# Attention with sinks and an ELU feed-forward on one core: another shape for the sinks' product, another place for one subtraction, and two operations that ScalarE may take

## The chip, the cores and the metric

One core of one Trainium2 chip. The metric is the device time of one execution in microseconds (us); below it is the median of several runs. TensorE (PE) multiplies, VectorE (DVE), ScalarE (ACT) and GpSimd (POOL) do the element work, SyncE (SP) issues the transfers.

## The reference

```python
# q, k, v: 4 batches x 8 heads x 768 positions x 64; n_sink 4, window 128
scores = scale * np.matmul(q, k.transpose(0, 1, 3, 2))
keep = is_sink | in_window            # 4 sinks, and the last 128 positions
a = np.exp(scores - max); a = a / (sum + 1e-09)
x = matmul(a, v)                      # tokens (4 x 768 = 3072) x 512
h = x @ w_in                          # 512 x 2048
g = np.where(h > 0.0, h, np.exp(np.minimum(h, 0.0)) - 1.0)
return g @ w_out                      # 2048 x 512
```

## The kernel before

The 3072 tokens are 24 tiles of 128, taken in nine chunks of 2, 2, 2 and then 3 tiles. A tile sees its own keys, those of the tile before it and, from the third tile of a batch on ("far"), the four sinks. For each chunk the four pairs of heads go through attention, which leaves x, and then 16 blocks f of the hidden layer go through the feed-forward. The order of the parts is: blocks 0 to 7 of chunk 0, blocks 0 to 7 of chunk 1, blocks 8 to 15 of chunk 0, blocks 8 to 15 of chunk 1, then all 16 blocks of each further chunk. The attention of a chunk runs between the blocks of the chunks ahead of it.

Numbers are kept in two 16-bit parts, a high and a low one, so a product takes three matmuls. In `feed_forward` the first product of a block (L783, "S1") is 12 matmuls into one half-used PSUM bank `h`; there are two such banks. ScalarE takes the exponential (L791) into `g` in SBUF, VectorE subtracts one and scales (L793), VectorE takes the larger of that and h (L794) into `g`, ScalarE rounds it to the high part `gh` (L796), GpSimd subtracts to get the low part `gl` (L797), and the second product (L804, "S2", 6 matmuls for two tiles) adds into the banks `acc`. The bank `h` is free for the second block after when L794 is done; S2 of a block stands some two blocks behind its S1.

The weights come as 32 pieces of 64-bit words `raw` that are turned into 32-bit numbers on the chip: ScalarE scales the upper word into the bank `acc` that is not yet in use (L274), the sign (L277 on VectorE or L275 on GpSimd) and the low bits (L278 on VectorE or L276 on GpSimd) go into `wu`, VectorE puts them together (L279), ScalarE rounds the high part (L428) and GpSimd subtracts for the low part (L429).

Chunks 0 and 1 have an attention of their own in 32-bit numbers, `attention_f32`: scores (L505, 64 rows for each head), the masked maximum (L512, VectorE), the exponential (L515, ScalarE), four turns on TensorE (L522, "turn"), the copy of the turned probabilities to `pt` (L526, ScalarE or VectorE), then in `values` the product with the values (L562) and a product that spreads the reciprocal of the sum (L568); these two write 64 rows of the bank `po` for each head. Chunk 1 alone of these is far: two small turns (L547) bring the sinks' eight columns into `po`, L550 copies them to eight rows of a `pq` tile, and L565 multiplies these 8 rows with 128 columns, both heads at once, between L562 and L568. Behind `values`, L581, L582, L584 and L585 make x, its high part on ScalarE and its low part on VectorE; the next S1 needs all four pairs. Chunk 2 and later have another attention (scores L679 in chunk 2, L673 and L674 later; values L743 and L748).

No order is written by hand: `Plan` holds every task with an engine (some with a second one), a duration, what it depends on, and, for TensorE, a position. `forward` places tasks engine by engine, the most urgent first, each at the engine that takes it earliest; what comes out is the order in which each engine's queue is recorded.

Of the kernel before, what the change touches and what calls it, by code (L numbers as in the profile page):

```python
# [45 lines left out]
LAG = 2  # L46
WHOLE = 3
# [3 lines left out]
RINGS = dict(kqs=2, kq=3, vs=2, vm=1, vhl=2, e=3, st=6, pq=3, pt=6, g=2, gh=3, x=7, wv=4, s=2, po=1, h=2, wu=2, sv=2, wps=1, raw=6, s4=4, tp=2, rx=2)  # L51
# [44 lines left out]
class Plan:  # L96
# [6 lines left out]
    PATIENCE, LEEWAY, ISSUED = 0.1, 5.0, 0.15  # L103

# [3 lines left out]
    def add(self, eng, dur, fn, *args, deps=(), lat=0.0, pos=None, or_=None, gap=1.75, port=None):  # L108

        t = Task(eng, dur, fn, args, deps, lat, pos, gap, port)  # L110
        if or_:
            t.ways[or_[0]] = or_[1:]
        self.tasks.append(t)
        return t
# [59 lines left out]
    def forward(self):  # L174
# [6 lines left out]
        lock = 0.0  # L181
# [11 lines left out]
        while done < len(self.tasks):  # L193
# [61 lines left out]
def dve_us(n):  # L255
    return 0.1 + 0.00104 * n
# [10 lines left out]
def weight_f32(nc, v, d, u, raw):  # L267
# [8 lines left out]
        "bits POOL": lambda: nc.gpsimd.tensor_scalar(ui[:, :, 0], halves[:, :, 1], 2.0**-13, -4095.5 / 8192, ALU.mult, ALU.add),  # L276
        "sign DVE": lambda: nc.vector.tensor_scalar(ui[:, :, 1], halves[:, :, 3], 0x8000, None, ALU.bitwise_and),  # L277
# [52 lines left out]
def fast_path(tc, ctx, first, kq, vx, wt, out, nw, flag, limits):  # L330
# [71 lines left out]
    def weights(k):  # L402
# [8 lines left out]
        def step(i):  # L411
            return lambda: weight_f32(nc, v, acc[2], wu[k % RINGS["wu"]], raw)[i]()

        ld = add("SP", 0.45, load, deps=[w_done.get(k - AHEAD, [None])[0]], lat=dma_us(P * 512 * 8))
        if wide:
            a = add("ACT", act_us(512) + 0.05, step("d"), deps=[ld])
            u1 = add("DVE", 0.34, step("sign DVE"), deps=[ld], or_=("POOL", 0.75, step("sign POOL")), port=True)
            u2 = add("DVE", 0.34, step("bits DVE"), deps=[u1], or_=("POOL", 0.85, step("bits POOL")), port=True)
# [45 lines left out]
    def attention_f32(c):  # L464
# [12 lines left out]
        for p in range(NP):  # L477
# [10 lines left out]
            for j, g in enumerate(ts):  # L488
# [18 lines left out]
                sc = add("PE", 0.75 if c else 0.65 if nb == 1 else 1.2, scores, deps=[ldk, *freed] if c and k < 1 else [ldk], pos=at[k])  # L507
# [33 lines left out]
            sk_ = sp = None  # L541
            if far:
                sp = pqs[slot("pq")].rearrange("p b k -> p (b k)").bitcast(F32)[0 : 2 * NS, :qc]
# [5 lines left out]
                sk_ = add("PE", 0.3, sinks, deps=[u for v in prods for u in (v[0], v[9])], pos=at[k - 1] + 2.5)  # L549
                cs = add("ACT", act_us(qc) - 0.03, lambda sp=sp, po=po: nc.scalar.activation(sp, po[0 : 2 * NS, :qc], AF.Copy), deps=[sk_], or_=("DVE", dve_us(qc) - 0.03, lambda sp=sp, po=po: nc.vector.tensor_copy(sp, po[0 : 2 * NS, :qc])))  # L550
# [3 lines left out]
            def values(po=po, vr=vr, sp=sp, prods=prods):  # L554
                for _, _, _, pt, rs, g, j, nb, _, _ in prods:
# [8 lines left out]
                    if far:  # L564
                        nc.tensor.matmul(po[:, oc], vr[0 : 2 * NS, nk * P : (nk + 1) * P], sp[:, oc], start=False, stop=False)  # L565
# [4 lines left out]
            val = add("PE", 0.2 + sum(0.22 * v[7] + 0.22 for v in prods), values, deps=[ldv, sk_, *[u for v in prods for u in v[:2]]], pos=at[k - 1] + 4.0)  # L570
# [3 lines left out]
            if far:  # L574
                ring("pq", [sk_], [val])
# [16 lines left out]
    def attention(c):  # L592
# [39 lines left out]
        for p in range(NP):  # L632
# [21 lines left out]
            for g in ts:  # L654
# [29 lines left out]
                else:  # L684
                    scs = [add("PE", 0.75, scores([0, 1]), deps=kqp[0][2:4], pos=at[k])] * 2
# [27 lines left out]
                if t >= 2:  # L713
# [8 lines left out]
                    b = add("POOL", 0.85, sinks, deps=[rr], port=False)  # L722
# [27 lines left out]
            val = add("PE", 0.16 + sum(0.16 * v[4] + (0.06 if v[5] >= 2 else 0.0) for v in prods), values, deps=[va, vb, *[v[0] for v in prods]], pos=at[k - 1] + V_AT)  # L750
# [4 lines left out]
            fa = add("ACT", act_us(qc), lambda xh=xh, po=po: nc.scalar.activation(xh, po[:, :qc], AF.Copy, scale=PO_SCALE), deps=[val])  # L755
            fb = add("DVE", dve_us(qc), lambda xh=xh, xl=xl, po=po: nc.vector.scalar_tensor_tensor(xl, po[:, :qc], PO_SCALE, xh, ALU.mult, ALU.subtract), deps=[fa])
# [375 lines left out]
```

## Time and profile before

| | us |
|---|---|
| median of 3 runs | 639.59 |
| lowest and highest | 638.42, 641.27 |
| profiled execution, its own time | 636.94 |
| its span, first to last instruction | 634.9 |
| TensorE busy in the span | 613.5 (97%) |
| VectorE, ScalarE, GpSimd busy | 429.7, 416.0, 366.1 |

The span is read in stretches: the attention of chunk 0 up to the first S1 at 30.8 us; the first part of chunk 0 with the attention of chunk 1 up to 76.7 us, where the first S1 of chunk 1 starts; the two parts behind it; the steady rest up to 628.2 us, and a tail. In the timeline's rows a matmul of 32-bit numbers counts as two instructions.

### The profile page before, as it was taken

To read this page: it belongs to the slowest core of one execution; us is meant where nothing else is said; L and a number is where in the kernel's file an instruction comes from. 1 tells how busy PE (TensorE), PEld (TensorE's weight loads), DVE (VectorE), ACT (ScalarE), POOL (GpSimd) and SP (SyncE) were. 2 spreads that over 40 slices of the span, in tenths; PEclk is the share of its full clock that TensorE was granted. 3 is DMA by queue.
4 is the path that set the end of the run, shared out by engine and by line. 5 is a ranking of instruction groups with operands and counts; after the bars stand their busy time and mean duration, and the time that the engine had idled before them with its cause. 6 is when DMAs were issued, how large, how long until landed. Compare 5 with 4: busy or idle time off the path is not lost.

```text
span 634.9 us, 13430 instructions
## 1 busy us (share of the span) xinstructions
PE 613.5 (97%) x4521; PEld 373.6 (59%) x4521; DVE 429.7 (68%) x1202; ACT 416.0 (66%) x1181; POOL 366.1 (58%) x617
## 2 busy tenths in 40 slices
PE   5799899999999999999999999999999999999995
PEld 3566566677776565555656565565555555555552
DVE  6989897777869666576666777676676967442222
ACT  5977878668888766666676766666667666432221
POOL 3778777865778665555656666655546674222221
PEclk9999999999999999999999999999999999999998
DMA  8764993555665754364535565464345624300001
GB/s 311 262 251 171 265 250 137 164 151 147 142 160 121 180 118 118 98 178 120 149 102 143 153 117 155 108 202 120 118 113 150 191 69 106 88 35 17 0 2 55
DMA packets 113517, 87.94 MB, mean 139 GB/s; under 512 B 88352, under 2 KB 93472, under 8 KB 113440
## 3 DMA queue, kind: packets, MB, share of 16 engines
q1 hardware_dynamic: 113296, 87.00, 49.4%
q8 instruction: 37, 0.61, 0.4%
q14 instruction: 40, 0.33, 0.2%
q10 hardware_dynamic: 144, 0.00, 0.0%
HBM read 58.41 MB, written 7.34 MB: 104 GB/s over the span
## 4 chain that ended last, share of the span: by engine, by line
PE 91%; DVE 4%; ACT 2%; issue 1%; DMA 1%; POOL 0%; DVEq 0%; ACTq 0%
PE h L783 39%; PE acc L804 39%; PE po L743 4%; PE s L674 3%; PE s L673 3%; ACT e L515 1%; DMA words<-in_words_dram 1%; PE po L562 1%; DVE wv L279 1%; DVE e L512 1%; DVE wu L278 1%; PE s L679 1%; PE po L565 1%; PE po L748 0%; PE po L568 0%
## 5 line engine op out<-in xcount | busy, mean ns | idle before, releaser
L783 PE MATMUL h<-x,w 128*128 128x384 f16 (+1 forms) x1728 | 273.2, 309 | 1.3 <-DVE g L794 1.3
L783 PEld LDWEIGHTS <-w 128*128 128x128 f16 x1728 | 164.4, 98 | 91.1 <-issue 2.7
L797 POOL TENSOR_TENSOR gl<-g,gh 128x384 f16<-128x384 f32 (+1 forms) x144 | 126.3, 878 | 155.0 <-ACT gh L796 120.4
L804 PE MATMUL acc<-w,gh 128*128 128x512 f16 x768 | 192.7, 380 | 0.0
L793 DVE TENSOR_SCALAR g<-g 128x384 f32<-128x384 f32 (+1 forms) x144 | 64.1, 445 | 122.5 <-ACT g L791 121.9
L796 ACT ACTIVATE gh<-g 128x384 f16<-128x384 f32 (+1 forms) x144 | 69.4, 482 | 76.5 <-DVE g L794 76.2
L804 PEld LDWEIGHTS <-gh 128*128 128x128 f16 x768 | 70.2, 98 | 70.6 <-issue 1.6
L710 DVE SCALAR_TENSOR_TENSOR pq<-e,st,pq 128x256 f16<-128x256 f32 x160 | 88.3, 583 | 33.9 <-ACT pq L709 33.5
L791 ACT ACTIVATE g<-h 128x384 f32<-128x384 f32 (+1 forms) x144 | 64.5, 448 | 69.9 <-PE h L783 60.1
L804 PE MATMUL acc<-w,gl 128*128 128x512 f16 x384 | 109.2, 379 | 0.1
L697 ACT ACTIVATE e<-e,st 128x264 f32<-128x264 f32 x160 | 78.0, 488 | 11.4 <-DVE st L695 9.8
L709 ACT ACTIVATE pq<-e,st 128x256 f16<-128x256 f32 x160 | 69.6, 479 | 6.9 <-DVE st L702 3.9
L794 DVE SCALAR_TENSOR_TENSOR g<-g,h 128x384 f32<-128x384 f32 (+1 forms) x144 | 72.3, 503 | 2.0
L695 DVE CUSTOM_DVE_ANT_0 e<-s,m 128x264 f32<-128x264 f32 x160 | 60.4, 405 | 13.7 <-PE s L674 12.4
L624 POOL TENSOR_TENSOR kq<-kqs,kq 128x396 fp32r<-128x396 f32 (+1 forms) x48 | 58.2, 1213 | 13.0 <-ACT kq L621 8.0
L804 PEld LDWEIGHTS <-gl 128*128 128x128 f16 x384 | 37.6, 98 | 45.8 <-POOL gl L797 0.6
L621 ACT ACTIVATE kq<-kqs 128x780 fp32r<-128x780 f32 (+1 forms) x48 | 42.7, 901 | 16.3 <-PE s L674 12.3
L625 POOL TENSOR_TENSOR kq<-kqs,kq 64x384 fp32r<-64x384 f32 x48 | 48.2, 1004 | 3.8
L673 PE MATMUL s<-kq 128*128 128x264 f32 (+1 forms) x144 | 50.0, 366 | 0.0
L701 POOL TENSOR_SCALAR st<-st 128x2 f32<-128x2 f32 x80 | 17.4, 218 | 43.4 <-ACT e L697 36.3
L429 POOL TENSOR_TENSOR w<-wv,w 128x512 f16<-128x512 f32 x32 | 38.3, 1197 | 5.6 <-ACT w L428 3.5
L674 PE MATMUL s<-kq 128*128 128x264 f32 (+1 forms) x144 | 37.8, 282 | 0.0
(120 smaller groups left out, 696.1 us busy)
## 6 DMA issues: line engine op xcount, KB each, us to landing
raw<-in_wt_dram SPq DMA_DIRECT2D x32, 512.0 KB, 5.4
kqs<-in_kq_dram SPq DMA_DIRECT2D x24, 456.0 KB, 3.5
kqs<-in_kq_dram SPq DMA_DIRECT2D x24, 390.0 KB, 3.2
out_dram<-wv SPq DMA_DIRECT2D x24, 256.0 KB, 2.9
vs<-in_vx_dram SPq DMA_DIRECT2D x20, 256.0 KB, 2.9
vm<-in_vx_dram SPq DMA_DIRECT2D x6, 768.0 KB, 4.7
vs<-in_vx_dram SPq DMA_DIRECT2D x12, 320.0 KB, 3.1
kqs<-in_kq_dram SPq DMA_DIRECT2D x8, 326.0 KB, 4.2
```

Source lines behind the costliest of these rows:

```text
L673: nc.tensor.matmul(sp[:, :wd], q, hi[:, c0 : c0 + wd], start=True, stop=False)
L695: red = add("DVE", 0.08 + 0.00104 * wd, lambda ee=ee, me=me, sp=sps[e], m=m, wd=wd: nc.vector.tensor_tensor_reduce(ee, sp[:, :wd], m[:, :w ...
L697: ex = add("ACT", act_us(wd, sums=True), lambda ee=ee, me=me, rs=rs[:, e : e + 1]: nc.scalar.activation(ee, ee, AF.Exp, bias=me, scale=-1. ...
L709: a = add("ACT", act_us(nb * P, True), lambda src=src, hi=hi, re=re: nc.scalar.activation(hi, src, AF.Copy, scale=re), deps=[rr])
L710: b = add("DVE", dve_us(nb * P) + 0.03, lambda src=src, hi=hi, lo=lo, re=re: nc.vector.scalar_tensor_tensor(lo, src, re, hi, ALU.mult, ALU ...
L783: nc.tensor.matmul(hp[:, :n], win[:, part, d, :], xx[:, :n], start=k == 0, stop=k == 3 * ND - 1)
L791: a = add("ACT", act_us(n) + 0.06, lambda gf=gf, hp=hp, sums=sums: nc.scalar.activation(gf, hp[:, :n], AF.Exp, scale=1.0 / G_SCALE, accum_ ...
L793: b = add("DVE", 0.07 + 0.00053 * n, lambda gf=gf: nc.vector.tensor_scalar(gf, gf, -1.0, G_SCALE, ALU.add, ALU.mult), deps=[a], port=True)
L794: b = add("DVE", dve_us(n), lambda gf=gf, hp=hp: nc.vector.scalar_tensor_tensor(gf, gf, 0.0, hp[:, :n], ALU.min, ALU.max), deps=[b])
L796: th = add("ACT", act_us(n), lambda gf=gf, gh=gh: nc.scalar.activation(gh[:, :n], gf, AF.Copy), deps=[b])
L797: tl = add("POOL", pool_us(n), lambda gl=gl, gf=gf, gh=gh: nc.gpsimd.tensor_tensor(gl[:, :n], gf, gh[:, :n], ALU.subtract), deps=[th])
L804: nc.tensor.matmul(acc[i], gg[:, i * P : (i + 1) * P], wout[:, part, :], start=f == f0 and k == 0, stop=f == f1 - 1 and k == 2)
```

## The change

1. In chunk 1 the sinks' eight rows are copied into the first 8 rows of a 128-row tile `sq` of zeros (two of them, cleared at the start by GpSimd), and the sinks' product is two matmuls of 128 rows by 64 columns, one for each head, of the same form as those beside it.
2. For chunk 0 (`NEAR`), L794 writes its result into the unused half of the bank `h` in place of `g`; ScalarE rounds from there, and VectorE in place of GpSimd subtracts from there for `gl`. The bank `h` is free only behind that subtraction, the tile `g` already behind the maximum.
3. ScalarE may take g's scaling (in all chunks) and the weights' low bits.
4. The planner's durations are renewed, and a matmul whose shape (`mode`) differs from that of the task ahead costs it 0.096 us more.

```diff
+NEAR = 1
+            if e == "PE":
+                s, mode = s + (self.SWITCH if t.mode != mode else 0.0), t.mode
...
+        "bits ACT": lambda: nc.scalar.activation(ui[:, :, 0], halves[:, :, 1], AF.Copy, scale=2.0**-13, bias=-4095.5 / 8192),
...
+    sqs = rows("sq", [P, SIZES[1] * P], F32)
+    for t in sqs:
+        nc.gpsimd.memset(t, 0.0)
...
-            u2 = add("DVE", 0.34, step("bits DVE"), deps=[u1], or_=("POOL", 0.85, step("bits POOL")), port=True)
+            u2 = add("DVE", 0.34, step("bits DVE"), deps=[u1], or_=[("POOL", 0.85, step("bits POOL")), ("ACT", 0.56, step("bits ACT"))], port=True)
...
-                        nc.tensor.matmul(po[:, oc], vr[0 : 2 * NS, nk * P : (nk + 1) * P], sp[:, oc], start=False, stop=False)
+                        for e in range(2):
+                            vo = nk * P + e * D
+                            nc.tensor.matmul(po[e * D : (e + 1) * D, oc], vr[:, vo : vo + D], sq[:, oc], start=False, stop=False)
...
+            near = 2 * n <= 512 and c < NEAR
+            gd = hp[:, n : 2 * n] if near else gf
+            if near:
+                tl = add("DVE", dve_us(n) - 0.035, lambda gl=gl, gd=gd, gh=gh: nc.vector.tensor_tensor(gl[:, :n], gd, gh[:, :n], ALU.subtract), deps=[th])
+                ring("h", [s1], [tl])
+            else:
+                tl = add("POOL", pool_us(n), lambda gl=gl, gd=gd, gh=gh: nc.gpsimd.tensor_tensor(gl[:, :n], gd, gh[:, :n], ALU.subtract), deps=[th])
+                ring("h", [s1], [b])
```

In the whole program GpSimd loses the 16 subtractions of chunk 0 and VectorE gets them; 44 of the 144 scalings go to ScalarE (19 of the 48 with 256 columns, 25 of the 96 with 384), and 8 of the 32 low bits (VectorE 21 to 14, GpSimd 11 to 10). TensorE's other work is the same.

The order moves on every engine. On TensorE, the values of the first pair of chunk 1 (`po` is the bank, `pt` the turned probabilities, `vs` the values, `st` the reciprocals). Before:

```order
L562 MATMUL po_164<-pt_99,vs_66 64x128 x4
L565 MATMUL po_164<-pq_94,vs_66 128x128
L568 MATMUL po_164<-ident,st_90 64x128 x2
L562 MATMUL po_164<-pt_100,vs_66 64x128 x4
L565 MATMUL po_164<-pq_94,vs_66 128x128
L568 MATMUL po_164<-ident,st_91 64x128 x2
```

and after:

```order
L571 MATMUL po_164<-pt_99,vs_66 64x128 x4
L576 MATMUL po_164<-sq_197,vs_66 64x128 x2
L579 MATMUL po_164<-ident,st_90 64x128 x2
L571 MATMUL po_164<-pt_100,vs_66 64x128 x4
L576 MATMUL po_164<-sq_197,vs_66 64x128 x2
L579 MATMUL po_164<-ident,st_91 64x128 x2
```

All matmuls of such a block now write 64 rows from 128 rows; the four pairs of chunk 1 are alike.

On TensorE at the end of the first part of chunk 0, where the last pair of chunk 1 is turned (`e_85` is its last tile, `s` a bank of chunk 2's scores). Before:

```order
L804 MATMUL acc_166<-w_143,gl_109 128x512
L522 MATMUL po_164<-ident,e_85 128x128 x4
L679 MATMUL s_162<-kqs_65 128x264
L679 MATMUL s_163<-kqs_65 128x264
L547 MATMUL po_164<-ident,st_90 8x128
L547 MATMUL po_164<-ident,st_91 8x128
L562 MATMUL po_164<-pt_99,vs_67 64x128 x4
```

and after:

```order
L530 MATMUL po_164<-ident,e_85 128x128 x4
L821 LDWEIGHTS gh_106
L821 MATMUL acc_165<-w_143,gh_106 128x512
L821 LDWEIGHTS gh_106
L821 MATMUL acc_165<-w_143,gh_106 128x512
L821 LDWEIGHTS gl_109
L821 MATMUL acc_165<-w_143,gl_109 128x512
L556 MATMUL po_164<-ident,st_90 8x128
L556 MATMUL po_164<-ident,st_91 8x128
L821 LDWEIGHTS gh_106
L821 MATMUL acc_166<-w_143,gh_106 128x512
```

The last second product of the part, two groups of three matmuls, moved: it stood ahead of the last turn and stands now between the turn, the small turns of the sinks and the values.

On ScalarE within the first part of chunk 0 (`acc<-raw` and `w<-wv` are weight steps, `e` probabilities, `rx` a step of x). Before:

```order
L428 ACTIVATE w_138<-wv_116 128x512
L274 ACTIVATE acc_167<-raw_127 128x512
L791 ACTIVATE g_104,checks<-h_161 128x256
L515 ACTIVATE e_86,st_89<-e_86,st_89 128x264 x2
L796 ACTIVATE gh_107<-g_103 128x256
L526 ACTIVATE pt_102<-po_164 128x512
L796 ACTIVATE gh_105<-g_104 128x256
```

and after:

```order
L281 ACTIVATE wu_120<-raw_126 128x512
L523 ACTIVATE e_85,st_88<-e_85,st_88 128x264
L808 ACTIVATE gh_107<-h_160 128x256
L802 ACTIVATE g_104,checks<-h_161 128x256
L278 ACTIVATE acc_167<-raw_126 128x512
L804 ACTIVATE g_104<-g_104 128x256
L523 ACTIVATE e_86,st_89<-e_86,st_89 128x264 x2
L436 ACTIVATE w_138<-wv_116 128x512
```

A low-bits step (L281) and a scaling (L804) joined ScalarE's queue, and the rounding L808 reads the bank `h`.

## Rows read from the trace of the kernel before

**Rows 1.** Busy time by stretch: us, engines busy (x instructions), TensorE's clock, DMA, GB/s.

```profile
7.70:30.80 23.10, 18.64 (x148) 12.58 (x149) 21.94 (x87) 22.53 (x73) 15.14 (x26) 1.00 0.84 320
30.80:76.70 45.90, 43.11 (x330) 27.58 (x328) 41.75 (x113) 36.54 (x104) 36.09 (x56) 1.00 0.68 226
76.70:118.40 41.70, 40.37 (x331) 27.95 (x331) 34.75 (x75) 32.67 (x94) 32.38 (x47) 1.00 0.62 178
143.40:628.20 484.80, 484.65 (x3513) 287.84 (x3507) 308.67 (x860) 306.63 (x861) 262.11 (x440) 1.00 0.45 115
```

**Rows 2.** Timeline, TensorE, values of chunk 1's second pair: start, us, engine, line, operation.

```profile
49.37 0.66 PE L562 MATMUL po<-pt,vs 128*64 128x128 f32 x8
49.96 0.48 PE L565 MATMUL po<-pq,vs 8*128 8x128 f32 x2
50.37 0.44 PE L568 MATMUL po<-ident,st 128*64 128x128 f32 x4
50.64 0.61 PE L562 MATMUL po<-pt,vs 128*64 128x128 f32 x8
51.17 0.48 PE L565 MATMUL po<-pq,vs 8*128 8x128 f32 x2
51.59 0.44 PE L568 MATMUL po<-ident,st 128*64 128x128 f32 x4
51.96 1.48 PE L783 MATMUL h<-x,w 128*128 128x256 f16 x12
```

**Rows 3.** Timeline, TensorE, values of chunk 0's last pair.

```profile
25.88 0.44 PE L562 MATMUL po<-pt,sv 128*64 128x128 f32 x4 [0.82 <-DVE x L585]
26.15 0.39 PE L568 MATMUL po<-ident,st 128*64 128x128 f32 x4
26.37 0.61 PE L562 MATMUL po<-pt,sv 128*64 128x128 f32 x8
26.80 0.39 PE L568 MATMUL po<-ident,st 128*64 128x128 f32 x4
27.12 0.72 PE L505 MATMUL s<-kqs 64*128 64x264 f32 x4
```

**Rows 4.** Timeline, TensorE, 67 to 82 us; in brackets the idle time ahead.

```profile
67.48 0.59 PE L804 MATMUL acc<-w,gh 128*128 128x512 f16 x2
67.91 0.38 PE L804 MATMUL acc<-w,gl 128*128 128x512 f16 x1
68.78 0.66 PE L522 MATMUL po<-ident,e 128*128 128x128 f32 x4 [0.49 <-DVE pt L526]
...
70.93 0.38 PE L547 MATMUL po<-ident,st 128*8 128x128 f32 x2 [0.75 <-DVE pt L526]
71.78 0.66 PE L562 MATMUL po<-pt,vs 128*64 128x128 f32 x8 [0.46 <-ACT pq L550]
...
74.36 0.72 PE L679 MATMUL s<-kqs 64*128 64x264 f32 x4
...
76.72 2.79 PE L783 MATMUL h<-x,w 128*128 128x256 f16 x24
...
81.74 1.47 PE L783 MATMUL h<-x,w 128*128 128x256 f16 x12 [1.33 <-DVE g L794]
```

**Rows 5.** Groups by shape, 30 to 100 us: operation xcount | busy us, mean ns | idle ahead.

```profile
L797 POOL TENSOR_TENSOR gl<-g,gh 128x256 f16<-128x256 f32 x16 | 11.8, 741 | 5.3 <-ACT gh L796 5.1
L278 DVE TENSOR_SCALAR wu<-raw 128x512 uint16<-128x512 uint16 x13 | 9.6, 754 | 0.0
L793 DVE TENSOR_SCALAR g<-g 128x256 f32<-128x256 f32 x16 | 9.0, 562 | 2.2 <-ACT g L791 2.1
L796 ACT ACTIVATE gh<-g 128x256 f16<-128x256 f32 x16 | 6.5, 409 | 3.7 <-DVE g L794 3.7
L428 ACT ACTIVATE w<-wv 128x512 f16<-128x512 f32 x20 | 12.4, 622 | 0.5 <-DVE wv L279 0.5
L585 DVE TENSOR_TENSOR x<-po,x 128x256 f16<-128x256 f32 x5 | 2.1, 417 | 0.3 <-ACT x L584 0.3
```

More of the change, by code (lines that the diff above doesn't have):

```diff
@@ L103, with add @@
     PATIENCE, LEEWAY, ISSUED = 0.1, 5.0, 0.15
+    SWITCH = 0.096
     def __init__(self):
         self.tasks, self.rings = [], {}
[L108 to L112, printed above, removed]
+    def add(self, eng, dur, fn, *args, deps=(), lat=0.0, pos=None, or_=(), gap=1.75, port=None, mode=None):
+        t = Task(eng, dur, fn, args, deps, lat, pos, gap, port, mode)
+        for way in or_:
+            t.ways[way[0]] = way[1:]
         self.tasks.append(t)
@@ L180, in forward @@
         dma = self.LOADED
-        lock = 0.0
+        lock, mode = 0.0, None
         def release(t):
@@ L505, in scores @@
                         nc.tensor.matmul(sps[e][:, :wd], st[r, qo : qo + P], st[r, c0 : c0 + wd], start=True, stop=True)
-                sc = add("PE", 0.75 if c else 0.65 if nb == 1 else 1.2, scores, deps=[ldk, *freed] if c and k < 1 else [ldk], pos=at[k])
+                sc = add("PE", 0.65 if c else 0.6 if nb == 1 else 1.0, scores, mode="rows", deps=[ldk, *freed] if c and k < 1 else [ldk], pos=at[k])
                 scored.append(sc)
@@ L568, in values @@
                         nc.tensor.matmul(po[e * D : (e + 1) * D, oc], rs[:, e : e + 1].to_broadcast([P, D]), ident, start=False, stop=end)
-            val = add("PE", 0.2 + sum(0.22 * v[7] + 0.22 for v in prods), values, deps=[ldv, sk_, *[u for v in prods for u in v[:2]]], pos=at[k - 1] + 4.0)
+            val = add("PE", 0.03 + 0.216 * sum(v[7] + 1 + far for v in prods), values, mode="columns", deps=[ldv, sk_, *[u for v in prods for u in v[:2]]], pos=at[k - 1] + 4.0)
             for cp, _, red, *_ in prods:
@@ L574, in attention_f32 @@
             if far:
-                ring("pq", [sk_], [val])
+                ring("sq", [sk_], [val])
             if held:
@@ L684, in attention @@
                 else:
-                    scs = [add("PE", 0.75, scores([0, 1]), deps=kqp[0][2:4], pos=at[k])] * 2
+                    scs = [add("PE", 0.65, scores([0, 1]), mode="rows", deps=kqp[0][2:4], pos=at[k])] * 2
                 if k < 1:
@@ L748, in values @@
                             nc.tensor.matmul(po[e * D : (e + 1) * D, oc], vhi[:, vo : vo + D], pt[:, 8, :], start=False, stop=end)
-            val = add("PE", 0.16 + sum(0.16 * v[4] + (0.06 if v[5] >= 2 else 0.0) for v in prods), values, deps=[va, vb, *[v[0] for v in prods]], pos=at[k - 1] + V_AT)
+            val = add("PE", 0.025 + sum(0.168 * v[4] + (0.056 if v[5] >= 2 else 0.0) for v in prods), values, mode="columns", deps=[va, vb, *[v[0] for v in prods]], pos=at[k - 1] + V_AT)
             for v in prods:
```

51 lines of the change are left out of this document (25 added, 26 removed).

## The prediction

> **What bounds the kernel now.** I read the busy time by stretch first: there one sees where TensorE's line is full. From 143.4 to 628.2 us it is busy 484.65 of 484.80 us at a granted clock of 1.00 [rows 1], so nothing that another engine does there can shorten the run; only less work on TensorE could, and the change takes none away there. Ahead of that TensorE is idle or thin in three stretches. Up to 30.8 us (A) it is busy 18.64 of 23.10, with ScalarE at 22.53 and VectorE at 21.94: these two set the pace. From 30.8 to 76.7 (B) it is busy 43.11 of 45.90, with VectorE at 41.75. From 76.7 to 118.4 (C) it is busy 40.37 of 41.70 [rows 1]. Then I read TensorE's own timeline for the block that is edited [rows 2] and its model in chunk 0 [rows 3], then its waits at the hand-over from B to C [rows 4], and last what the moved instructions cost [rows 5].
>
> The whole run's time is the end of TensorE's line plus a fixed tail, so the change is worth what it takes from TensorE's work and waits up to 118 us. All sums are made on the profiled execution, 636.94 us (span 634.9). The median of the runs is 639.59, 2.65 above it; I carry the difference over to the median unchanged.
>
> **The sinks' product (the sure term).** A block of values in chunk 1 takes from 49.37 to 51.96, 2.59 us [rows 2]. In it each 8-row step stands for 0.41 us (49.96 to 50.37, and 51.17 to 51.59) though it is only two of the trace's instructions, and the 0.59 and 0.53 us of the eight instructions ahead of it are also longer than the 0.43 of the same eight in chunk 0 (26.37 to 26.80), where no other shape follows [rows 2, 3]. So the price lies in the two changes of shape, not in the product. After the change all is of one shape: 0.48 for the first eight (0.43 and the 0.05 by which the first four of chunk 0, 25.88 to 26.15, exceed the 0.22 of half of 0.43), 0.22 for the four new ones, 0.22 for the reciprocals, then 0.43, 0.22, and 0.32 with the way out (26.80 to 27.12) [rows 3]: 1.89 us. That is 0.70 less, and four pairs make **2.8 us**. The form of the new matmul is that of its neighbours, so I bound the term narrowly: 2.2 (if each new pair took the 0.27 of 25.88 to 26.15 and its neighbours 0.1 more) to 3.1.
>
> The Trainium skill, TensorEngine Tiling (Array Packing), Key Properties, says that a change of the tiling mode drains TensorE; these rows agree. Its section When to Use Tiling says that a contraction of 32 rows or fewer may be tiled four times, which speaks for the 8 rows and against 128; by that rule the change gives a cheap form up, which is a rival below.
>
> The copies to `sq` are the old copies with another target. The two clearings by GpSimd stand at the start, where it has nothing urgent: no cost; were they in the way, one 128x512 instruction of 0.6 us would be a generous price.
>
> **Stretch A.** I count in the two orders what stands ahead of the last step of x in chunk 0. On ScalarE seven instructions of 512 columns less (two scalings of weights, three roundings, two copies of turned tiles) and one exponential less, one low-bits step more: 7 x 0.62, 0.41 and 0.62 [rows 5], together 4.1 us less. On VectorE two low-bits steps less, one sign more at 0.754 [rows 5], and two copies for two assemblies of the same width: 0.75 less. VectorE now is the fuller of the two, so the lower number rules: I take **1.0**, between 0.75 and 4.1 and close to the first; the range is 0.5 lost (the order of the pairs' tiles changes, and a turn may wait) to 2.5 won.
>
> **Stretch B.** TensorE has 2.8 us less, if its feeders follow. ScalarE gets four scalings (0.41) and four instructions of 512 columns more (0.62), and two narrower ones less (0.41): +3.3, to 39.8 us. VectorE gets eight subtractions (0.417) and loses four scalings (0.562) and six bit steps (0.754): -3.4, to 38.3. GpSimd loses eight subtractions, 5.9 of 36.09 [rows 1, 5]. A stretch of 42 us holds both, ScalarE at 95%. At the hand-over TensorE waits 0.49, 0.75 and 0.46 [rows 4]. In the new order three matmuls stand between the last turn and the small turns, and three between those and the values; three take 0.65 (67.48 to 67.91 is two, 0.43) [rows 4]. They cover most of 0.75 and 0.46, and the first turn's copy has more work ahead of it too. The copies' own length stays, so I take **0.8** of these 1.7, range 0 to 1.7. The way from the last values to the first S1 of chunk 1, 74.36 to 76.72 [rows 4], is rounding and subtracting on two engines; it stays, with chunk 2's scores beside it as before.
>
> **Stretch C.** The 1.33 us ahead of 81.74 is the third S1, which waits for a bank `h` until L794 of the first is done [rows 4]. The new order puts scores there in place of values and takes the bit steps off VectorE; I leave this wait as it is. ScalarE is what I fear. Between the exponentials of the 9th and the 24th block it has eight more scalings (0.41), ten more instructions of 512 columns (0.62; five are low bits) and six more of some 256 (0.41): +12.0 on 32.67, more than the 40.4 us of TensorE [rows 1, 5]. About half of it is weight and attention work drawn ahead from the stretch behind, for which nobody waits yet, and S2 stands two blocks behind its S1. I put **+0.5** there, range 0 to 4.
>
> Behind 143 us 25 scalings move to ScalarE, which is busy 306.63 of 484.8 [rows 1]: nothing. The tail keeps its order.
>
> **Sum.** -2.8 - 1.0 - 0.8 + 0.5 = -4.1 us: 632.8 on the profiled execution, 635.5 on the median.
>
> **Rivals.**
>
> *Work off, wait on.* TensorE's 2.8 us come back as waits, since ScalarE is filled: B and C then take what ScalarE takes. It has 36.54 + 32.67 + 3.3 + 12.0 = 84.5 us to do in them; at the 97.5% that it reached in A (22.53 of 23.10) that is 86.7, against 87.6 before [rows 1]. With the gain in A that is -1.9: 637.7, within the half per cent. For it: the count of C. Against it: part of C's work may come later without harm.
>
> *More than the sum.* A shrinks by what both feeders lose (2.5), the waits of B go (1.7), C costs nothing: -7.0, 632.6. For it: VectorE and GpSimd lose more than TensorE. Against it: in A the two engines feed each other in turns, and TensorE's waits end on their chain, not on their sum.
>
> *The bank is held too long (slower).* In chunk 0 the bank `h` now is free behind the rounding on ScalarE and the subtraction on VectorE, not behind L794. In C the first S1 ends about 78.03 (half of 76.72 to 79.34) and its bank is free at 81.7 [rows 4]: 3.7 us. Rounding and subtracting add 0.41 and 0.42 [rows 5] and two queues; with 0.5 us at each queue the bank is held 5.5. Between the end of an S1 and the start of the next but one stand an S1 and two S2 (1.3 each) and, now and then, scores (0.65): 3.9 to 4.6. Seven pairs of blocks would each wait about 1.2 us: +8.4 on the sum, 643.9. It decides once the bank is held longer than 4.6 us. Against it: in the first part, where the blocks of chunk 0 run with the attention, no S1 waits for a bank in the trace.
>
> *Eight rows were the cheap form.* If the count of instructions decided and not the changes of shape, 16 more instructions of 0.055 would add 0.9 us to TensorE, and the sum is -1.3 + 0.9 = -0.4: 639.2. That is where the rule on small contractions leads. The 0.41 us of the 8-row steps speak against it [rows 2].
>
> **How the numbers follow.** Forecast 0.50, 635.5. More than the sum 0.14. Work off, wait on 0.22. Bank held 0.10. Eight rows 0.04. About 0.5%, 3.2 us, is what a measurement of this kernel can tell from no change. Faster by more than that is below 636.4: all of the second case and some four fifths of the forecast's, 0.55. Slower is above 642.8: 0.09 of the bank's 0.10. The rest, 0.36, lies within. The range goes from 632.0, just beyond the second case, to 640.5, so that it holds the third and the fifth with the spread of the runs; the bank's case is left out, and some of the best.
>
> **What the profile after would show.** The sinks' step: blocks of values of chunk 1 in 1.9 us, with no row of 8 rows in them. A: the first S1 about 29.8. B: the first S1 of chunk 1 at about 72, and waits at the hand-over of about 0.9 in all. C: ScalarE above 95% busy; were it the bound, S1 or S2 would wait for L808 or for the exponentials. The bank: S1 waiting for L810. The forecast is wrong if the blocks of values still take over 2.2 us, if chunk 1 starts after 75, or if TensorE shows more than 3 us of idle time between 76 and 143.

## The result and the profile after

| | before | after |
|---|---|---|
| median, runs of the first comparison | 639.0 us (4 runs) | 631.63 us (4 runs, 631.15 to 633.66) |
| ratio, 95% interval | | 0.9884 [0.985, 0.9918] |
| profiled execution, its own time | 636.94 | 631.99 |
| its span | 634.9 | 630.1 |
| first S1 / first S1 of chunk 1 | 30.82 / 76.72 | 29.10 / 69.94 |

The change is 7.4 us faster at the median and 4.95 us between the two profiled executions. Forecast were 4.1 on both. The direction was right; on the median 631.63 lies just below the forecast's range (632.0 to 640.5), while on the profiled execution 631.99 stands 0.8 below the 632.8 of the sum.

First the busy time by stretch of the kernel after (columns as in [rows 1]). The stretches are again A up to the first S1, B up to the first S1 of chunk 1, C, and the steady rest.

```profile
7.70:29.10 21.40, 18.72 (x148) 13.32 (x149) 18.75 (x84) 19.20 (x64) 11.26 (x22) 1.00 0.79 293
29.10:69.94 40.84, 39.62 (x342) 26.60 (x340) 37.65 (x107) 38.20 (x110) 32.72 (x51) 1.00 0.73 245
69.94:113.00 43.06, 41.36 (x352) 27.87 (x352) 37.95 (x88) 41.65 (x118) 35.55 (x50) 1.00 0.75 232
138.00:622.90 484.90, 484.74 (x3510) 287.78 (x3505) 299.38 (x833) 319.83 (x895) 262.12 (x441) 1.00 0.46 115
```

A is 1.72 us shorter and B 5.06; what is behind the first S1 of chunk 1 is 1.98 longer (630.1 less 69.94, against 634.9 less 76.72). VectorE, at 41.75 of 45.90 in B before [rows 1], has 37.65 of 40.84, and GpSimd 32.72 in place of 36.09 (columns: TensorE, its weight loads, VectorE, ScalarE, GpSimd). ScalarE took the load: 38.20 in B, and 41.65 of 43.06 in C.

The values of chunk 1's first pair, TensorE's timeline (start, us, operation), answer [rows 2]:

```profile
33.20 0.66 PE L571 MATMUL po<-pt,vs 128*64 128x128 f32 x8
33.69 0.39 PE L576 MATMUL po<-sq,vs 128*64 128x128 f32 x4
33.91 0.39 PE L579 MATMUL po<-ident,st 128*64 128x128 f32 x4
34.12 0.61 PE L571 MATMUL po<-pt,vs 128*64 128x128 f32 x8
...
35.10 1.48 PE L794 MATMUL h<-x,w 128*128 128x256 f16 x12
```

The block takes 1.90 us (33.20 to 35.10) where 2.59 stood; 1.89 was forecast. The hand-over from B to C, same view, answers [rows 4]; the first row is one of the kernel before that [rows 4] leaves out:

```profile
75.72 1.06 PE L679 MATMUL s<-kqs 64*128 64x264 f32 x4 [0.64 <-DVE st L695]
```

```profile
64.33 0.38 PE L556 MATMUL po<-ident,st 128*8 128x128 f32 x2 [0.20 <-DVE pt L534]
...
67.26 0.72 PE L690 MATMUL s<-kqs 64*128 64x264 f32 x4
68.95 1.06 PE L690 MATMUL s<-kqs 64*128 64x264 f32 x4 [0.97 <-DVE st L706]
69.94 2.79 PE L794 MATMUL h<-x,w 128*128 128x256 f16 x24
72.67 0.72 PE L690 MATMUL s<-kqs 64*128 64x264 f32 x4
74.85 2.80 PE L794 MATMUL h<-x,w 128*128 128x256 f16 x24 [1.47 <-DVE g L807]
```

The three waits ahead of the last values have shrunk from 1.70 us to one of 0.20; ahead of the last scores 0.97 stands where 0.64 stood. One scores step (0.65 us) that stood in B is now at 72.67, in C. The wait for the bank `h` of chunk 1, which has no new subtraction, is there as before: 1.47 in place of 1.33.

### The profile page after: what moved, and what is told of

The parts are those of the page before. It is cut to its first block, busy times and chain, and to the rows that moved or that the text cites. A ratio compares the mean times of both kernels' runs of the same rounds, so it can differ in the third digit from the quotient of the medians.

```text
span 630.1 us, 13434 instructions
## 1 busy us (share of the span) xinstructions
PE 611.1 (97%) x4537; PEld 373.8 (59%) x4537; DVE 411.7 (65%) x1167; ACT 434.5 (69%) x1231; POOL 356.1 (57%) x604
## 4 chain that ended last, share of the span: by engine, by line
PE 82%; ACT 3%; issue 1%; POOL 1%; DVE 0%; POOLq 0%; DVEq 0%; ACTq 0%
PE h L794 36%; PE acc L821 36%; PE po L754 4%; PE s L685 3%; PE s L684 3%; ACT acc L278 1%; PE po L759 0%; ACT g L802 0%; ACT w L436 0%; ACT pq L720 0%; POOL gl L813 0%; ACT wu L281 0%; ACT g L804 0%; POOL w L437 0%; ACT gh L808 0%
## 5 line engine op out<-in xcount | busy, mean ns | idle before, releaser
L794 PE MATMUL h<-x,w 128*128 128x384 f16 (+1 forms) x1728 | 273.7, 309 | 1.7 <-DVE g L807 1.5
L794 PEld LDWEIGHTS <-w 128*128 128x128 f16 x1728 | 164.6, 98 | 92.2 <-issue 3.5
L813 POOL TENSOR_TENSOR gl<-g,gh 128x384 f16<-128x384 f32 (+1 forms) x128 | 113.8, 890 | 147.7 <-ACT gh L808 133.4
L804 DVE TENSOR_SCALAR g<-g 128x384 f32<-128x384 f32 (+1 forms) x100 | 43.7, 437 | 127.6 <-ACT g L802 127.1
L808 ACT ACTIVATE gh<-g 128x384 f16<-128x384 f32 (+1 forms) x128 | 62.8, 491 | 69.7 <-DVE g L807 69.3
L708 ACT ACTIVATE e<-e,st 128x264 f32<-128x264 f32 (+1 forms) x160 | 77.8, 487 | 6.7 <-DVE st L706 6.4
L807 DVE SCALAR_TENSOR_TENSOR g<-g,h 128x384 f32<-128x384 f32 (+1 forms) x128 | 66.1, 516 | 7.1 <-ACT g L804 4.6
L706 DVE CUSTOM_DVE_ANT_0 e<-s,m 128x264 f32<-128x264 f32 (+1 forms) x160 | 59.7, 405 | 13.5 <-PE s L685 12.6
```

Of the source, the lines that this page charges most:

```text
L706: red = add("DVE", 0.08 + 0.00104 * wd, lambda ee=ee, me=me, sp=sps[e], m=m, wd=wd: nc.vector.tensor_tensor_reduce(ee, sp[:, :wd], m[:, :w ...
L708: ex = add("ACT", act_us(wd, sums=True), lambda ee=ee, me=me, rs=rs[:, e : e + 1]: nc.scalar.activation(ee, ee, AF.Exp, bias=me, scale=-1. ...
L794: nc.tensor.matmul(hp[:, :n], win[:, part, d, :], xx[:, :n], start=k == 0, stop=k == 3 * ND - 1)
L807: b = add("DVE", dve_us(n) - 0.035, lambda gf=gf, gd=gd, hp=hp: nc.vector.scalar_tensor_tensor(gd, gf, 0.0, hp[:, :n], ALU.min, ALU.max), ...
L808: th = add("ACT", act_us(n) - (0.03 if near else 0.0), lambda gd=gd, gh=gh: nc.scalar.activation(gh[:, :n], gd, AF.Copy), deps=[b])
L813: tl = add("POOL", pool_us(n), lambda gl=gl, gd=gd, gh=gh: nc.gpsimd.tensor_tensor(gl[:, :n], gd, gh[:, :n], ALU.subtract), deps=[th])
```

## The experiments

Each kernel was timed beside the kernel before on the same chip; the ratio is to that. These sets are e1 to e4, e5 to e8, e9 to e11 and e12 to e14, and the kernel before had medians of 639.4, 641.2, 638.7 and 639.4 in them, so medians of different sets compare less well than those of one set. The three columns of stretches come from each one's profiled execution: the start of the first S1, from there to the first S1 of chunk 1, and the rest of the span.

| kernel | median us | ratio [95%] | A | B | rest |
|---|---|---|---|---|---|
| before, first profile | 639.59 | | 30.82 | 45.90 | 558.18 |
| e1 before again | 639.49 | 1.0006 [0.9982, 1.0029] | 31.74 | 48.84 | 560.02 |
| after, first profile | 631.63 | 0.9884 [0.985, 0.9918] | 29.10 | 40.84 | 560.16 |
| e7 after again | 631.5 | 0.9872 [0.9845, 0.99] | 28.47 | 40.80 | 559.83 |
| e2 product alone | 638.88 | 0.9996 [0.9975, 1.0018] | 32.75 | 43.80 | 560.65 |
| e3 eight rows back | 634.0 | 0.9914 [0.9882, 0.9947] | 28.48 | 42.58 | 560.14 |
| e4 numbers alone | 636.47 | 0.9957 [0.9934, 0.9981] | 30.22 | 44.44 | 561.34 |
| e5 near off | 634.55 | 0.9915 [0.989, 0.9941] | 28.68 | 43.74 | 559.78 |
| e6 ScalarE's ways off | 641.73 | 1.003 [1.0009, 1.0051] | 31.93 | 44.42 | 561.55 |
| e11 old numbers | 640.44 | 1.002 [0.9998, 1.0041] | 32.05 | 46.40 | 560.55 |
| e12 ways back in place | 641.72 | 1.0042 [1.0021, 1.0063] | 28.85 | 43.25 | 566.70 |
| e13 near back in place | 636.73 | 0.9963 [0.9943, 0.9983] | 28.68 | 43.69 | 562.03 |
| e8 after, fillers at the start | 630.13 | 0.9842 [0.9817, 0.9867] | 31.16 | 40.78 | 558.76 |
| e14 the same again | 630.95 | 0.987 [0.9841, 0.9899] | 28.00 | 40.83 | 559.27 |
| e9 before, fillers | 638.18 | 1.0 [0.9982, 1.0019] | 31.91 | 45.79 | 559.40 |
| e10 after, more fillers | 631.57 | 0.9887 [0.9861, 0.9913] | 28.69 | 40.89 | 560.42 |

### Is 636.94 the kernel before? (e1, e7)

Both kernels unaltered.

> The kernel before, unchanged, once more: its runs are what the change is measured against, and they were 638.4 to 641.3 us where its profiled execution was 636.94. If the difference is the granted clock, runs near 639 show a mean clock of about 0.993 to 0.995 where the profiled one showed 0.997, and their spans follow the clock (0.002 of 635 us is 1.3 us). If it is the stretch up to 31 us (which order the engines' waits fall in), the clocks agree and the first S1 of a slower profile stands later than 30.82. If the first profile was only a lucky one, a new profile comes out near 639.

> The changed kernel unaltered. Its four times so far are 631.2 to 633.7, with a median of 631.6. Theory of the clock (runs of the kernel before spread over 6 us because TensorE's granted clock falls behind TensorE's waits near 31 and 75 us in about half of them; the changed kernel waits less there): most runs at 631 to 632 with a mean clock above 0.995, and the few with a lower clock some 2 us above. Rival (four lucky runs): a median of 633 or more and a spread of 4 us or more.

In 108 runs of the kernel before (e1's 12 and the 96 timed beside the experiments) the times go from 636.4 to 642.6, with a median of 639.4. They sort by the mean granted clock of TensorE: 38 runs below 0.9925 have a median of 641.8, 56 runs of 0.9955 or more one of 638.0. The first profile (636.94) was among the fastest there are. Not all of its lead is clock: four runs of e1 at 638.7 to 639.0 had its mean clock of 0.997 or more, and what sets them apart from it stays open. e1's own profile shows what the runs at a low clock do. Two stretches of e1 (columns as above; the clock is the number ahead of the DMA's share), and then the same stretches of the kernel after:

```profile
31.00:34.20 3.20, 3.20 (x16) 2.46 (x17) 2.10 (x8) 1.40 (x3) 2.65 (x4) 0.50 0.82 277
75.20:85.30 10.10, 9.57 (x47) 5.89 (x44) 6.12 (x20) 6.82 (x19) 5.24 (x12) 0.50 0.92 291
```

```profile
31.00:34.20 3.20, 3.20 (x37) 2.49 (x37) 2.92 (x9) 3.20 (x13) 2.46 (x5) 1.00 0.96 351
75.20:85.30 10.10, 10.10 (x95) 7.05 (x93) 8.43 (x20) 10.07 (x29) 7.51 (x10) 1.00 1.08 305
```

In e1 the clock is at its lower level (1.2 GHz, 0.50) for both stretches, and each stands right behind waits of TensorE (0.67 and 0.29 us at 29.0 and 30.8, not shown, ahead of the first). e1's timeline at the hand-over:

```profile
70.80 0.66 PE L522 MATMUL po<-ident,e 128*128 128x128 f32 x4 [0.49 <-DVE pt L526]
...
72.96 0.38 PE L547 MATMUL po<-ident,st 128*8 128x128 f32 x2 [0.75 <-DVE pt L526]
73.80 0.66 PE L562 MATMUL po<-pt,vs 128*64 128x128 f32 x8 [0.46 <-ACT pq L550]
...
80.58 5.16 PE L783 MATMUL h<-x,w 128*128 128x256 f16 x24
```

They are the very waits of [rows 4], and two S1 take 5.16 us where 2.79 stood. The kernel after waits less there, and in its 10 runs (630.92 to 633.78, median 631.5) none has a clock below 0.9925. So part of the gain at the median is, by these runs, clock that the kernel before loses in a third of its runs; no row of its first profile could show that, since its clock read 1.00 in every stretch of [rows 1].

### The product by itself (e2, e3)

```diff
-    nc.tensor.matmul(po[:, oc], vr[0 : 2 * NS, ...], sp[:, oc], ...)
+    for e in range(2):
+        nc.tensor.matmul(po[e * D : (e + 1) * D, oc], vr[:, vo : vo + D], sq[:, oc], ...)
```

e2 puts this into the kernel before with its order unchanged (and three clearings by GpSimd at the start, done at 3.2 us, long before its next work); e3 takes it back in the kernel after, with its order unchanged.

> The kernel before with the 128-row sinks' product alone; every engine's order is that of before. If TensorE's line sets the pace from 31 to 68 us, blocks of values take 1.9 us in place of 2.59, the run is 2.0 to 2.8 us faster and the first S1 of chunk 1 stands at about 74.2. If VectorE and ScalarE set it there, the waits at the hand-over grow by what the blocks lose, the first S1 of chunk 1 stays at 76 or later, and the run is less than 1 us faster.

> The changed kernel with the 8-row sinks' product put back; every engine's order is that of the changed kernel. Product as a term of its own: 2.0 to 2.8 us slower than the changed kernel (some 634.2 on the median), blocks of values at 2.59. If the moves of work are what gave the time, and TensorE has room, under 1 us slower than the changed kernel.

In the new order the product is worth 2.4 us (634.0 against 631.6), near the 2.8 of the sum. In the old order it is worth nothing that these runs can tell; at a clock of 0.9955 or more e2's median is 638.6, the kernel before's 638.0. e2's stretches from the first S1 of chunk 1 to 143 us and behind, and then those of the kernel before:

```profile
76.55:143.00 66.45, 63.29 (x505) 43.03 (x505) 52.38 (x122) 46.98 (x139) 49.40 (x74) 1.00 0.61 179
143.00:637.20 494.20, 487.35 (x3535) 289.59 (x3533) 311.48 (x867) 308.47 (x867) 262.61 (x443) 1.00 0.46 115
```

```profile
76.72:143.00 66.28, 64.95 (x519) 44.26 (x518) 53.49 (x125) 48.60 (x144) 50.94 (x76) 1.00 0.62 178
```

B was 2.10 us shorter in e2 (43.80 against 45.90): the product's time did come off. But behind it TensorE is idle for 3.16 us (66.45 less 63.29) where it had been idle for 1.33. Two rows of e2's timeline hold 2.62 of that:

```profile
80.59 0.30 PE L749 MATMUL po<-pt,vh 128*64 128x128 f16 x4 [0.73 <-DMA pt<-pq]
83.06 1.47 PE L789 MATMUL h<-x,w 128*128 128x256 f16 x12 [1.89 <-DVE g L800]
```

TensorE came earlier to work that its feeders had not finished. The second case of e2's expectation had the size but not the place: the waits at the hand-over stayed (0.60, 0.74 and 0.46), and the time went behind it. This is read from one execution, and the second of these waits varies: its counterpart was 1.47 and 1.96 us in the two profiles of the kernel after. (A was 1.9 us longer in this execution: its matmuls ran at half speed until later, six turns taking 1.44 us at 15.61 where the kernel before has 0.87 at 14.13. That is the clock's spread again and not the edit.) The forecast's rival that eight rows were the cheap form is dead: in the new order they cost 2.4 us more than 128. The Trainium skill, TensorEngine Tiling (Array Packing), When to Use Tiling, would tile so small a contraction, and its Key Properties name a drain of TensorE at a change of mode. These runs agree with such a price for the change of shape, but none shows the drain by itself.

### The planner's numbers (e4, e11)

e4 is the kernel before with the renewed durations and the price of a change of shape alone; e11 is the kernel after with the old ones:

```diff
-    SWITCH = 0.096
+    SWITCH = 0.0
...
-    sc = add("PE", 0.65 if c else 0.6 if nb == 1 else 1.0, scores, ...)
+    sc = add("PE", 0.75 if c else 0.65 if nb == 1 else 1.2, scores, ...)
```

> The kernel before with the planner's renewed durations and its price for a change of shape alone: old product, chunk 0's subtraction on GpSimd, no new work for ScalarE. If a better order alone wins the 1.7 us ahead of the first S1 and the waits at the hand-over, it is 1.5 to 3.5 us faster than before. If those need the work taken off VectorE, it is within 1 us of before.

> The changed kernel with the planner's durations of the kernel before and no price for a change of shape; the product, near and ScalarE's two ways stay. The renewed durations alone, without those three, gave 3.0 us. Theory 1 (durations near the measured ones place the tasks better whatever the rest): 633.5 to 636, most of the 3.0 lost. Theory 2 (the renewed durations only matter where VectorE is short, and ScalarE's ways make it free): 631 to 632.5.

Alone the numbers gain 3.0 us, inside the 1.5 to 3.5 of e4's first case. Without them all the other parts together gain nothing: 640.44, a ratio of 1.002. In e11's profile A is 32.05 and B 46.40, as long as before, although the product and the moved steps are in it. Theory 2 of e11 is refuted; theory 1 forecast only the loss of the 3.0, and 9 went, so neither had it.

### The moved steps: planned anew (e5, e6) and in place (e12, e13)

e5 sets `NEAR = 0`. e6 takes the two `or_` ways of ScalarE out. In both the planner makes a new order.

> The changed kernel with NEAR = 0: GpSimd subtracts for gl in chunk 0 again, from g in SBUF; the product on 128 rows, the planner's numbers and ScalarE's two new ways stay. The planner's numbers alone gave 636.5 with the 8-row product; with the new product that is some 634.1 (2.4 less, as the eight rows put back showed), and the whole change gives 631.6, so near and ScalarE's ways hold 2.5 us together. Theory 1 (VectorE is the bound of the first 77 us, so what is taken off it counts): ScalarE's ways carry it, near adds work to VectorE: 631 to 632.3, with the first S1 of chunk 1 at 70 us or earlier. Theory 2 (the slow subtraction on GpSimd, 741 ns, is the chain that delays S2 and x): near carries it: about 634, with S2 waiting for L797's counterpart on GpSimd.

> The changed kernel without ScalarE's two new ways: every scaling of g is VectorE's and the low bits are VectorE's or GpSimd's; near and the product on 128 rows stay. Theory 1 (VectorE is the bound): 634 to 636, since near puts 16 subtractions on VectorE and nothing is taken off; the first S1 of chunk 1 at 73 us or later. Theory 2 (GpSimd's subtraction is the chain): 631.6 to 632.3.

e5 costs 3.0 us against the kernel after. e6 costs 10.2 and is no faster than the kernel before (1.003). e5 came out where theory 2 put it, e6 on theory 1's side and beyond its 634 to 636: neither had both. Near has a worth of its own, and without ScalarE's ways, near and the rest gain nothing. Since the order changed with each edit, e12 and e13 keep the order of the kernel after and only put the operations back on the engine where they had been (e13 likewise, with GpSimd and `g`):

```diff
+        for t in self.tasks:
+            if t.eng == "ACT" and next(iter(t.ways)) == "DVE":
+                t.take("DVE")
```

> The changed kernel in its own order, but each of the 44 scalings and 8 low-bits steps that ScalarE had taken is issued by VectorE at the same place of the order. Nothing is planned anew. Without ScalarE's ways and planned anew it was 641.7, 10 us slower than the changed kernel. Theory of the load (VectorE is short of time in the first 120 us): most of the 10 us come back, 637 to 642, with waits for VectorE at the hand-over. Theory of the order (the planner's new order lost the time, not the place of the operations): 631.5 to 634.

> The changed kernel in its own order, but g's low part in chunk 0 is subtracted by GpSimd from g in SBUF, at the same place of the order. Nothing is planned anew; planned anew it was 634.5, 3 us slower than the changed kernel. Theory of the load (VectorE's 0.42 us in place of GpSimd's 0.74 us, and a shorter way to S2): 633 to 635. Theory of the order: 631.2 to 632.2.

Both times the load theory holds; e12 came out inside its 637 to 642, e13 1.7 us beyond its 633 to 635. With the same order, 52 steps back on VectorE cost 10.2 us, and 16 subtractions back on GpSimd cost 5.2. Where e12 loses, by its stretch B and its waits behind it:

```profile
28.85:72.10 43.25, 40.33 (x342) 26.99 (x340) 42.94 (x113) 35.99 (x104) 32.90 (x51) 1.00 0.69 232
```

```profile
104.13 2.19 PE L797 MATMUL h<-x,w 128*128 128x256 f16 x12 [2.38 <-DVE gl L813]
...
119.30 1.47 PE L797 MATMUL h<-x,w 128*128 128x256 f16 x12 [1.26 <-DVE gl L813]
```

VectorE is busy 42.94 of 43.25 us, and S1 waits for the bank `h` until the new subtraction is done. This is the mechanism of the forecast's slow rival, "the bank is held too long", in two waits of 3.6 us together and not in the seven of 1.2 that it forecast; behind the first of them the matmuls run at half speed as well (2.19 us for an S1 of 1.47). It is ScalarE's ways that keep it away in the kernel after, where its only trace is 0.23 us at 98.87. e12's VectorE just ahead of that wait, and GpSimd beside it (timeline), show what a step costs there:

```profile
96.14 1.40 DVE L285 TENSOR_SCALAR wu<-raw 128x512 uint16<-128x512 uint16 x1
...
98.04 0.96 DVE L286 TENSOR_SCALAR wu<-raw 128x512 uint16<-128x512 uint16 x1
...
102.63 0.45 DVE L286 TENSOR_SCALAR wu<-raw 128x512 uint16<-128x512 uint16 x1
```

```profile
95.81 1.42 POOL L440 TENSOR_TENSOR w<-wv,w 128x512 f16<-128x512 f32 x1
97.19 1.48 POOL L816 TENSOR_TENSOR gl<-g,gh 128x256 f16<-128x256 f32 x2
...
102.79 0.77 POOL L282 TENSOR_SCALAR wu<-raw 128x512 f32<-128x512 f32 x1 [0.83 <-DVE wv L287]
```

The sign at 96.14 and the low bits at 98.04 end 0.31 and 0.33 us behind the end of the GpSimd instruction that ran beside them (97.23 and 98.67). The low bits at 102.63 began while GpSimd was idle and took 0.45.

e13's loss is elsewhere: S2 waits for GpSimd's subtraction, and behind the hand-over S1 runs at half speed (4.45 us for two, 2.80 in the kernel after).

```profile
66.68 0.39 PE L825 MATMUL acc<-w,gl 128*128 128x512 f16 x1 [1.16 <-POOL gl L814]
...
77.56 4.45 PE L797 MATMUL h<-x,w 128*128 128x256 f16 x24 [1.75 <-DVE g L810]
```

### TensorE's clock by itself (e8, e14, e9, e10)

```diff
+    nc.tensor.matmul(s_ps[0][:, 384:512], ones, ones, start=True, stop=True)
```

28 of these stand ahead of the first scores; e8 and e14 have six more behind the second scores, e10 58 at five later waits and e9 76 at eleven. Nobody reads them.

> The changed kernel with 28 matmuls of 128x128 16-bit numbers, all ones, into an unused corner of a scores bank ahead of the first scores, and six more behind the second scores. Nothing reads them. Up to about 13.5 us of its profile the changed kernel's matmuls run at half speed (a scores row of 1.60 us in place of 1.06). Theory of the clock (it rises some time after TensorE began to work): half speed ends about 3 us earlier, the first S1 starts at 28 to 28.8 in place of 29.1, the median falls by 0.3 to 1.2 us to 630.4 to 631.3. Rival (the rise goes by the launch, or the first 13 us are bound by transfers and by VectorE anyway): first S1 at 29.1 or later, median unchanged or up to 0.5 us slower from fillers in the way.

> The changed kernel with 28 matmuls of ones ahead of the first scores and six behind the second, as once before (630.1, most runs 629.8 to 630.5, while the version with more fillers gave 631.6 and none 631.5). If the gain is real: 629.8 to 630.6 again, at a mean clock above 0.995, and a first S1 at 27 to 28 us in the profile. If it was luck: 631 to 632.

> The kernel before, with matmuls of 128x128 16-bit ones into an unused part of a bank, which nobody reads: 28 ahead of the first scores and 2 to 12 at each of eleven places up to 82 us where TensorE waits, each group shorter than its wait. No other instruction is changed. Theory of the clock (the kernel before spreads from 636.4 to 642.6 because the granted clock rises late in some runs and falls to half behind the waits near 31 and 75 us in about half of them): no run falls to half near 31 or 75 us, the mean clock is above 0.995 in nearly all runs, the median comes to the fast end, 635.5 to 638, and the spread to 3 us. Rival 1 (the spread comes from transfers or VectorE, and the clock only follows): median and spread as before, 639 to 641.5. Rival 2 (the fillers get in the way): slower, 642 or more.

> The changed kernel with such matmuls ahead of the first scores (28), behind the second scores (9) and at four more waits up to 75 us (6 to 20). In the run with fillers at the start alone the granted clock rose at 4.4 us already, but fell to half again at 7.8 and 21.4 us in the profiled execution, behind the waits of 1.30 and 1.73 us. Theory of the clock: with those waits filled it stays full from about 5 us on, the first S1 starts at 27.5 to 28.5 us, the median is 628.5 to 630 (630.1 with fillers at the start alone, 631.5 without). Rival (the first 30 us are VectorE's and ScalarE's, whatever TensorE's clock): first S1 at 28.5 to 29 and a median of 630 to 631.5.

The clock does rise earlier. e8's timeline:

```profile
1.75 3.16 PE L900 MATMUL s<-ones 128*128 128x128 bf16 x28 [1.75 <-POOL ones L379]
5.19 0.50 PE L513 MATMUL s<-kqs 64*128 64x132 f32 x4 [0.27 <-DMA kqs<-in_kq_dram]
5.52 0.61 PE L513 MATMUL acc<-kqs 64*128 64x264 f32 x4
7.43 0.49 PE L900 MATMUL s<-ones 128*128 128x128 bf16 x6 [1.30 <-DVE st L520]
7.85 1.55 PE L513 MATMUL acc<-kqs 64*128 64x264 f32 x4
```

Three rows of the kernel after:

```profile
5.75 1.09 PE L513 MATMUL acc<-kqs 64*128 64x264 f32 x4
7.77 1.60 PE L513 MATMUL acc<-kqs 64*128 64x264 f32 x4 [0.93 <-DVE st L520]
...
23.79 1.06 PE L513 MATMUL s<-kqs 64*128 64x264 f32 x4 [0.22 <-DVE st L520]
```

The second scores take 0.61 us in e8, 1.09 in the kernel after. Behind the wait of 1.30 the clock has fallen again (1.55), in this profile, which is the slowest of e8's six runs (632.60); in e14's it stayed up and the first S1 stands at 28.00. In time this is worth little. e8 and e14 together have a median of 630.3 (12 runs), 1.2 below the kernel after (10 runs), and A counted from the first scores is 23.05 us in e14 where the kernel after has 23.95 and 23.64. But e10, which fills more waits, has 631.57, with its first S1 at 28.69, as e10's rival said. That VectorE and ScalarE set the pace of A does not follow, since e10's own fillers stand in the way. Its timeline, and then e14's:

```profile
19.50 1.28 PE L901 MATMUL h<-ones 128*128 128x128 bf16 x20 [1.34 <-DVE pt L534]
20.70 0.44 PE L571 MATMUL po<-pt,vm 128*64 128x128 f32 x4
```

```profile
19.92 0.44 PE L571 MATMUL po<-pt,vm 128*64 128x128 f32 x4 [1.74 <-DVE x L596]
```

Up to 17.3 us the two run alike; then the values that e14 begins at 19.92 begin behind the 20 fillers, 0.78 later, which is all of the difference between 28.00 and 28.69. What a clock held throughout would give is not shown. e9 narrows the kernel before somewhat (637.2 to 641.2; one run of 12 below 0.9925, against a third of all runs without fillers, but 4 of 23 in e9's own set), yet its median, 638.2, is no lower than that of the runs at full clock without fillers (638.0), and its ratio is 1.0. So the fillers take off some of the spread at most, and give no speed. e8 is the fastest kernel of these runs, by about 1 us; how much of that is real stays open.

## Why the forecast was right in direction and too small

*The product, -2.8.* Right at its place: 1.90 us a block. (Its lower bound comes to 2.0 and not 2.2 by the words beside it; nothing hangs on that.) Called "the sure term", it was not sure by itself: without the new order nothing is left of it at the end (e2).

*Stretch A, -1.0, measured -1.72 (-2.35 in e7's profile).* Here a step failed. I counted the steps that leave VectorE (0.75 us) and took the lower of two bounds because "VectorE now is the fuller of the two". It is not: VectorE is busy 18.75 us and ScalarE 19.20. VectorE's busy time fell by 3.2 (21.94 to 18.75), not by 0.75, and ScalarE's by 3.3, where 4.1 was counted. Groups by shape, VectorE, 7.7 us to the first S1 (xcount, busy us, mean ns), before and then after:

```profile
L278 DVE TENSOR_SCALAR wu<-raw 128x512 uint16<-128x512 uint16 x5 | 3.6, 718 | 0.0
...
L277 DVE TENSOR_SCALAR wu<-raw 128x512 uint16<-128x512 uint16 x5 | 2.9, 576 | 0.1
```

```profile
L282 DVE TENSOR_SCALAR wu<-raw 128x512 uint16<-128x512 uint16 x5 | 2.3, 464 | 0.5 <-DMA raw<-in_wt_dram 0.4
...
L283 DVE TENSOR_SCALAR wu<-raw 128x512 uint16<-128x512 uint16 x2 | 0.9, 444 | 0.0
```

Not only are there fewer low-bits steps: each that stays takes 444 ns in place of 718, and each sign 464 in place of 576. GpSimd's busy time in A fell as well, from 15.14 to 11.26. I priced steps at a mean of the old kernel, as if it were a property of the step. The Trainium skill, SBUF — State Buffer, Who interferes with whom, says that a tensor_scalar on VectorE can enter a mode that uses two ports, and that an instruction in such a mode and one on GpSimd shut each other out for a whole instruction. The rows of e12 agree, where the slow steps end some 0.3 us behind GpSimd's; no run shows the mode of these steps, and none varied GpSimd's load alone, so for A this cause is argued and not shown.

*Stretch B, -2.8 - 0.8, measured -5.06.* TensorE has 3.49 us less work there (43.11 to 39.62): 2.8 and the scores of 0.65 that went to C. Its idle time fell from 2.79 to 1.22, 1.57 in place of 0.8; the ceiling named for it was 1.7. The three waits named gave 1.50, the wait ahead of the last scores took 0.33 back, and 0.40 came from smaller gaps. The load count was right: VectorE is relieved, ScalarE at 38.20 of 40.84 holds.

*Stretch C and behind, +0.5, measured +1.98.* The 0.65 of scores came back, idle time up to 143 us rose from 1.33 to 1.70 (73.06 less 71.36), and the tail behind TensorE's last matmul from 6.7 to 7.2.

```profile
69.94:143.00 73.06, 71.36 (x581) 48.61 (x580) 56.22 (x141) 60.63 (x180) 50.29 (x76) 1.00 0.62 187
```

The remaining half microsecond I can't put to a row. B and C together are 3.08 us shorter, and 3.1 was forecast. That is luck in part: the gain of B and the cost of C were each put some 1.5 too small, of which 0.65 is the same scores in both. ScalarE as the bound, which I feared, did not come: it is busy 41.65 of 43.06, but TensorE's only two waits up to 143 us, 1.47 and 0.23, end on VectorE.

*The median: the step that failed most.* It is "I carry the difference over to the median unchanged". Carried over were 2.65 us (639.59 less 636.94). Measured, the median of the kernel after lies 0.36 below its profiled execution (631.63 against 631.99). These 3.0 us are most of the 3.9 between 635.5 and 631.63; the sum itself missed by 0.85 (4.95 against 4.1), nearly all of it in A. The profiled execution of before, with its clock at 1.00 in every stretch read, lay 2.43 us below the median of 108 runs; that of after lies 0.49 above the median of its 10 runs. 4.95, 2.43 and 0.49 make the 7.9 between these medians. Of the 2.43, 1.36 goes with the clock (the runs at 0.9955 or more are that much below all runs) and 1.07 is where that one execution lay among those. So most of what I missed is in a baseline of one execution, and not in a term of the sum.

*The rivals.* "More than the sum" has the nearest number on the median, 632.6 against 631.63, but by luck: the same -7.0 puts the profiled execution at 629.9, 2.1 below the 631.99 measured, where the sum's 632.8 is 0.8 above. Its arguments (A shrinks by more, the waits of B go) hold in part, while C was not free. "Work off, wait on" is what e2 shows for the product in the old order. "The bank is held" is, in part, what e12 shows without ScalarE's ways. Both were mechanisms that exist, kept away by another part of the same change.

*What the sum hid.* Taken out of the kernel after, the product costs 2.4, near 3.0 to 5.2, ScalarE's ways 10.2 and the numbers 8.9: some 25 us, for a gain of 7.9. The parts don't add; what one is worth hangs on the others: near without ScalarE's ways ends no faster than the kernel before, the product without the new order gives nothing, the numbers give 3.0 alone and 8.9 with the rest. My sum got near by costing the finished order, not the parts.

## What to carry to other kernels

Where an order is planned, cost the whole new order against the engines' busy share in each stretch, and don't credit an edit by itself: the same edit gave 2.4 us in one order and nothing in the other. Price a VectorE step by the range in which it was seen, and look at what GpSimd does beside it. Before carrying a profiled execution's difference to the median, look at several runs and their granted clock: TensorE's waits may be paid for twice, once as idle time and once as half speed behind them.

## What the runs showed of the hardware

TensorE begins at about half speed in every profile without fillers: the first full-length scores take 1.60 us, the same ones 1.06 later on (the clock column reads 1.00 there; it is the matmuls' own times that show it). Work that nobody reads, ahead of the first data, can bring the full clock forward: 0.61 in place of 1.09 us at 5.5 us in e8, e9 and e14, but 1.09 still in e10 behind the same 28 fillers. Behind the waits of 0.49, 0.75 and 0.46 us at the hand-over the clock fell to half in e1's execution (10.1 us at 0.50) and not in the first profile of the same program, where the waits were equally long, so one profile says little of it. And the price of a wait there was not its length: two S1 took 5.16 us in place of 2.79.
